# Three entries moved in a hand-written instruction order: a product of decays, a cumulative sum and a store in the fifth unit's stage

## The chip, the cores and the metric

The kernel runs on one core of a Trainium2 chip. The metric is the device time of one execution in microseconds (us). Before the change the median of three runs is 170.76 us, from 170.74 to 170.88 us.

## The reference, cut to what matters

For 4 batches and 8 heads a 48 by 48 state is carried over 768 tokens; every row of the state decays by its own factor alpha. The result, 3072 tokens of 384 numbers, goes through two matrix products with a squared ReLU between them.

```
state = alpha[:, :, t, :, None] * state + einsum('bhd,bhe->bhde', k[:, :, t], v[:, :, t])
y[:, :, t] = einsum('bhd,bhde->bhe', q[:, :, t], state)
...
h = x @ w_in            # 3072 x 384 by 384 x 2048
g = relu(h) * relu(h)
out = g @ w_out         # 2048 x 384
```

## The kernel before, in words

The work is cut into 12 units of 256 tokens each: `units` runs over three stretches of the sequence, and within a stretch over the four batches. Units are numbered from 0, so the fifth unit is unit 4 and the sixth is unit 5. A partition holds two neighbouring tokens. Names of operations end in the unit's number.

A unit's **front** (from unit 2 on, `decays_by_pair`) works as follows. Four loads bring alpha, k, q and v (`lda`, `ldk`, `ldq`, `ldv`, line 463). VectorE, or GpSimd for some units, multiplies the alphas of a token pair (`pr`, L570). ScalarE takes the logarithm of the product (`ln`, L573) and of the odd token's alpha (`lm`, L612). TensorE sums the logarithms over the tokens (`m1i`, a triangular matrix, L579, and four small matmuls, L582) into the bank `psW`, the first of the three banks of `psWH`. ScalarE takes three exponentials of that bank (`ei` L590, `ea` L592, `ec` L595); VectorE makes the other token's factors from them (`bk` L599, `lb` L614), ScalarE one more exponential (`es`, L616). VectorE multiplies k and q by the factors (`ekm` L646, `eqm0` and `eqm1` L641), into the tile `qks`. Two DMA transposes on SyncE's queue (`tr0`, `tr1`, L657) write the transposed tile `kqt`.

The **attention** part is one group on TensorE that makes the scores and the state's increment (`p0`, L877 and L730), two masked copies on VectorE (`mk`, L894) and a group for the output (`y`, L757 and L765). ScalarE and VectorE copy the output to the tile `xbf` (`xe` L911, `xf` L913). It is transposed (`xt`: for units 0 to 3 by TensorE, L929, with a copy to the tile `xt` on VectorE, `xv` L941, the "mix copy" here, or on ScalarE, L943; from unit 4 on by a DMA, L935).

The **dense** part makes eight groups of 12 matmuls for a unit's first layer (`s1_unit_0` to `_7`, L992). Their results go in turn to two banks, so that each group needs the copy of the group two before it to be done. That copy is the ReLU (`re`, L1000 on ScalarE or L1002 on VectorE), and the squares follow (`sq`, L1010, L1013, L1014). The second layer has two rows of tokens of four groups of four matmuls (`s2_unit_row_0` to `_3`, L1038), gathered in the bank `psO`, copied out by `oe` (L1045, L1047) to the tile `osb` and stored by `out` (L1054).

The order on each engine is written out by hand in `TABLES`, one list of names for each engine. `arrange` takes the operations in exactly this order, and `place` sets semaphore waits where an operation needs a result of another engine or of a DMA. An engine works through its list in order; it does not pass an instruction that waits. Which bank or buffer a group uses is set where the operation is made and not by its place in the list.

The place of the change is the stretch in which unit 2's dense part begins, unit 1's second layer ends and unit 4's front is made. There ScalarE's list reads `... xf2 xe2 lm4 ln4 vc3 ei4 ea4 ec4 re2_0 re2_1 es4 oe1_0 ...` (`vc3` copies unit 3's v to bf16, L637). The kernel ends with the last unit's second layer (`last_tile`, L953) and its stores.

Of the kernel before, what the change touches and what calls it, by code (L numbers as in the profile page):

```python
# [26 lines left out]
class Program:  # L27
# [145 lines left out]
    def emit(self):  # L173
# [48 lines left out]
        zero zlinc zlstr zident zcaus zcaus1 zla0 zla1 zones zown zown0 zown1 zqk0 zqk1 zqk2 zlb0 zlb1 ekm0_0  # L222
        eqm0_0 ekm1_0 eqm1_0 et10_0 mk0_0 sa0 mk1_0 ekm1 eqm0_1 eqm1_1 xv0 et1_1 sc0 mk1_1 mk0_1 sc1 re0_2 xf1
        sq0_3 xv1 pr2 sq0_5 re0_7 re1_0 lb2 re1_1 ekm2 eqm0_2 eqm1_2 sq0_7 re1_5 et1_2 sq1_1 sq1_5 re1_7 mk1_2
        pr3 sc2 mk0_2 lb3 eqm1_3 eqm0_3 ekm3 xv2 pr4 sq1_7 bk4 lb4 ekm4 eqm1_4 eqm0_4 sq2_1 mk1_3 mk0_3 sc3
        oe1_1 sd3 sq2_7 sq2_6 xf3 lb5 ekm5 eqm1_5 eqm0_5 sa4 mk1_4 mk0_4 re3_2 pr6 sc4 sq3_1 xf4 sq3_3 re3_5
        sq3_6 lb6 ekm6 sa5 mk0_5 sc5 mk1_5 eqm0_6 eqm1_6 oe3_0 xf5 sq4_1 re4_5 pr7 sq4_3 sq4_7 sq4_5 bk7 lb7
        eqm0_7 sa6 eqm1_7 ekm7 sc6 sd6 mk0_6 mk1_6 pr8 oe4_1 xf6 sq5_3 bk8 lb8 ekm8 sq5_5 sq5_6 sa7 mk0_7 sc7
# [8 lines left out]
        +256 +256 tr01_0 p0_0 tr11_0 kv0 +512 +512 +512 +256 +256 p1_0 m11 +512 +256 y0 +512 +512 +256 tr0_1 xt0  # L237
        tr1_1 s1_0_0 p0_1 s1_0_1 s1_0_3 s1_0_2 s1_0_4 y1 s1_0_5 xt1 s1_0_6 s1_0_7 s1_1_0 m1i2 s1_1_1 s1_1_2
        s1_1_3 s1_1_4 s1_1_5 tr0_2 s1_1_6 tr1_2 s2_0_0_0 s1_1_7 p0_2 s2_0_0_1 s2_0_0_2 s2_0_1_0 s2_0_1_1 m1i3
        s2_0_1_2 s2_0_0_3 s2_0_1_3 y2 s2_1_0_0 s2_1_0_1 xt2 s2_1_0_2 s1_2_0 s1_2_1 m1i4 s2_1_0_3 s1_2_2 s1_2_3  # L240
        s2_1_1_0 s1_2_4 s2_1_1_1 s1_2_5 p0_3 s2_1_1_2 s1_2_6 s1_2_7 s2_1_1_3 y3 m1i5 s2_2_0_0 s2_2_0_1 xt3
        s2_2_0_2 s2_2_0_3 s1_3_0 p0_4 s2_2_1_0 s2_2_1_1 s2_2_1_2 s2_2_1_3 s1_3_2 s1_3_1 y4 s1_3_4 s1_3_3 m1i6
        s1_3_6 s1_3_5 s2_3_0_0 s2_3_0_1 s1_3_7 p0_5 s2_3_0_2 s1_4_0 s1_4_1 s2_3_0_3 s1_4_2 s1_4_3 y5 s2_3_1_0
# [15 lines left out]
        vc10  # L259
    """,  # L260
    "sp": """
        lda0 ldk0 ldq0 ldv0 lda1 ldk4 ldq4 tr0_3 tr1_3 lda5 ldv4 tr0_4 tr1_4 out0_1 ldv5 lda6 ldk6 tr1_5 out1_1
        tr0_5 xt4 ldq6 ldv6 lda7 ldq7 ldk7 tr0_6 tr1_6 out2_1 xt5 ldv7 lda8 ldk8 out3_1 tr0_7 tr1_7 out4_1 xt6
        ldq8 ldv8 lda9 ldq9 ldk9 tr0_8 tr1_8 xt7 ldv9 lda10 out5_1 ldk10 tr0_9 tr1_9 out6_1 xt8 ldq10 ldv10
        lda11 ldk11 tr0_10 tr1_10 out7_1 xt9 ldq11 ldv11 tr0_11 tr1_11 xt10 out8_1 xt11 out9_1 out10_1 out11_0
# [852 lines left out]
```

## Time and profile before

| What | Before |
|---|---|
| Median of three runs | 170.76 us (170.74 to 170.88) |
| The profiled execution's own time | 171.26 us |
| Its span, first to last instruction | 169.5 us |
| Time outside the span | 1.76 us |
| TensorE matmuls, share of the span | 163.8 us, 97% |
| VectorE | 118.0 us, 70% |
| ScalarE | 109.6 us, 65% |
| GpSimd | 35.3 us, 21% |
| Granted TensorE clock | 1.0 of full speed |

A profile shows one execution. "PE" is TensorE, "PEld" its weight loads, "DVE" VectorE, "ACT" ScalarE, "POOL" GpSimd, "SP" SyncE; "SPq" and "POOLq" are rows in which the engine's queue issues a DMA. In a row of the timeline stand the start in us from the span's start, the duration, the engine, the line of the code, the operation with what it writes and reads, and in square brackets the idle time of the engine just before it with what ended it. Matmuls overlap in the pipeline: a row's duration reaches past the start of the next one, so lost time on TensorE is read from start to start. A DMA's landing is its start and the time to landing that the list of DMA issues gives.

### The profile page before, as it was taken

What the parts mean: (1) busy time and instruction counts of PE and PEld (TensorE: products, weight loads), DVE (VectorE), ACT (ScalarE), POOL (GpSimd) and SP (SyncE); (2) the same over time, 40 slices, a digit from 0 to 9 for tenths busy, and PEclk for the clock granted to TensorE, in tenths of its full rate; (3) what the DMA queues carried; (4) which work ended last, traced back from release to release, by engine and by line L of the source; (5) the groups of instructions that cost most, each with busy time, mean ns of one, the idle gap of its engine ahead of it and who ended that gap; (6) DMA issues with size and microseconds to landing.
All of it is one profiled execution on the core that took longest, in us unless ns stands there. A gap on an engine that the chain in (4) does not pass through costs nothing.

```text
span 169.5 us, 5392 instructions
## 1 busy us (share of the span) xinstructions
PE 163.8 (97%) x2369; PEld 125.9 (74%) x2369; DVE 118.0 (70%) x206; ACT 109.6 (65%) x212; POOL 35.3 (21%) x46
## 2 busy tenths in 40 slices
PE   7988999999799999999999999999999999999994
PEld 2556889767686697877778876788797788787773
DVE  6577899985849868975978977887969637342130
ACT  3968778786868388667477757375677374466440
POOL 4671879130172032100240000000600000000000
DMA  5999999989999998999989999979797761040012
GB/s 137 324 318 188 260 312 215 293 288 252 185 220 329 241 181 197 307 137 243 301 195 247 263 152 258 207 194 288 145 190 205 97 119 58 0 141 4 33 60 93
DMA packets 68407, 33.37 MB, mean 197 GB/s; under 512 B 63520, under 2 KB 65312, under 8 KB 68384
## 3 DMA queue, kind: packets, MB, share of 16 engines
q1 hardware_dynamic: 62784, 24.39, 65.6%
q0 software_dynamic: 3520, 7.87, 18.6%
q10 hardware_dynamic: 2080, 0.79, 1.8%
q8 instruction: 18, 0.29, 0.7%
q14 instruction: 5, 0.04, 0.1%
HBM read 25.17 MB, written 4.72 MB: 176 GB/s over the span
## 4 chain that ended last, share of the span: by engine, by line
PE 83%; DMA 12%; ACT 1%; POOL 1%; issue 1%; DVE 0%; SPq 0%
PE psO L1038 34%; PE psWH L992 33%; DMA raw<-in_alpha_dram 6%; DMA raw<-in_v_dram 3%; DMA raw<-in_k_dram 2%; PE psX L877 2%; PE psZ L765 2%; PE psX L953 2%; PE psWH L1038 2%; PE psWH L730 1%; PE psZ L877 1%; PE psX L765 1%; PE psO L992 1%; PE psWH L579 1%; POOL raw L463 1%; ACT rr L1000 1%
## 5 line engine op out<-in xcount | busy, mean ns | idle before, releaser
L992 PE MATMUL psWH<-xt,win 128*128 128x256 bf16 x552 | 70.5, 273 | 0.9 <-ACT rr L1000 0.9
L1038 PE MATMUL psO<-wout,gt 128*128 128x384 bf16 x352 | 67.0, 326 | 0.0
L992 PEld LDWEIGHTS psWH<-xt,win 128*128 128x128 bf16 x552 | 59.8, 114 | 7.4 <-ACT rr L1000 1.4
L1000 ACT ACTIVATE rr<-psWH 128x512 bf16<-128x512 f32 x79 | 46.5, 599 | 25.3 <-PE psWH L992 24.0
L1038 PEld LDWEIGHTS psO<-wout,gt 128*128 128x128 bf16 x352 | 32.7, 98 | 16.7 <-DVE gt L1010 0.2
L1010 DVE TENSOR_TENSOR gt<-rr 128x1024 bf16<-128x1024 bf16 (+1 forms) x46 | 26.6, 584 | 22.4 <-ACT rr L1000 22.4
L1013 POOL TENSOR_TENSOR gt<-rr 128x1024 bf16<-128x1024 bf16 x3 | 5.7, 1911 | 56.6 <-ACT rr L1000 56.6
L894 DVE TENSOR_TENSOR pm<-psZ,caus 128x1024 bf16<-128x1024 f32 x12 | 14.6, 1216 | 3.7 <-PE psWH L730 3.0
L1045 ACT ACTIVATE osb<-psO 128x384 f32<-128x384 f32 x17 | 8.4, 492 | 11.6 <-PE psO L1038 11.2
L894 DVE TENSOR_TENSOR pm<-psX,caus 128x1024 bf16<-128x1024 f32 x12 | 14.6, 1215 | 0.9 <-PE psX L877 0.5
L641 DVE TENSOR_TENSOR qks<-raw,eq 128x384 bf16<-128x384 f32 x22 | 11.4, 550 | 1.1 <-ACT eq L616 1.0
L646 DVE TENSOR_TENSOR qks<-raw,ek 128x768 bf16<-128x768 f32 x11 | 10.5, 950 | 1.1 <-ACT ek L558 1.0
L1002 DVE TENSOR_SCALAR rr<-psWH 128x512 bf16<-128x512 f32 x13 | 8.8, 683 | 1.2 <-PE psWH L992 1.2
L1014 ACT ACTIVATE gt<-rr 128x512 bf16<-128x512 bf16 (+1 forms) x11 | 8.9, 821 | 0.6 <-DVE rr L1002 0.4
L573 ACT ACTIVATE lab<-prd 128x384 bf16<-128x384 f32 x10 | 5.2, 522 | 6.0 <-DVE prd L570 5.8
L1086 PE MATMUL psO<-zero 128*128 128x512 bf16 (+1 forms) x27 | 7.7, 418 | 1.3 <-DVE zero L382 1.3
L913 DVE CAST xbf<-psZ 128x384 bf16<-128x384 f32 x10 | 5.5, 554 | 3.4 <-PE psZ L757 3.2
L850 POOL TENSOR_TENSOR sbd<-tmp,acm 128x192 bf16<-128x192 f32 x5 | 2.9, 588 | 20.6 <-DVE tmp L840 16.2
L911 ACT ACTIVATE xbf<-psX 128x384 bf16<-128x384 f32 x11 | 5.4, 490 | 2.4 <-PE psZ L757 2.3
L637 ACT ACTIVATE vbf<-raw 128x768 bf16<-128x768 f32 x7 | 5.9, 837 | 1.2 <-DMA raw<-in_v_dram 1.2
L570 DVE TENSOR_TENSOR prd<-raw 128x384 f32<-128x384 f32 x9 | 6.4, 707 | 0.2 <-DMA raw<-in_alpha_dram 0.2
L616 ACT ACTIVATE eq<-la 128x384 f32<-128x384 f32 x10 | 5.2, 522 | 2.0 <-DVE la L614 2.0
(130 smaller groups left out, 190.8 us busy)
## 6 DMA issues: line engine op xcount, KB each, us to landing
out_dram<-osb SPq DMA_DIRECT2D x11, 384.0 KB, 3.3
raw<-in_alpha_dram SPq DMA_DIRECT2D x9, 384.0 KB, 5.5
raw<-in_v_dram SPq DMA_DIRECT2D x9, 384.0 KB, 4.4
raw<-in_k_dram SPq DMA_DIRECT2D x8, 384.0 KB, 5.7
raw<-in_q_dram SPq DMA_DIRECT2D x8, 384.0 KB, 4.0
win<-in_moe_w_in_dram POOLq DMA_DIRECT2D x4, 384.0 KB, 8.8
wout<-in_moe_w_out_dram POOLq DMA_DIRECT2D x4, 384.0 KB, 8.9
raw<-in_k_dram POOLq DMA_DIRECT2D x3, 384.0 KB, 6.4
```

Of the source, the lines that this page charges most:

```text
L570: add("dve", lambda e: e.tensor_tensor(hd(PRD[la][:]), al(0), al(1), ALU.mult), dve_ns(HD), p0, reads=[("raw", r, 0)], writes=[("prd", la) ...
L641: add("dve", lambda e, j=j, dst=dst: e.tensor_tensor(dst, RAW[r][:, 2, :, j, :].rearrange("p (n x) d -> p n x d", x=2), EQ[la][:, j].rearr ...
L646: add("dve", lambda e, a=a, E=E: e.tensor_tensor(QKS[qs][:, a, :, :, 0:D], RAW[r][:, 1 + a].rearrange("p h j d -> p j h d"), E[la][:].rear ...
L894: add("dve", lambda e, hf=hf, psT=psT: e.tensor_tensor(PM[pm][:, hf].rearrange("p r n j t -> p (r n) (j t)"), psT[:, :, :].rearrange("p r ...
L992: ins = pe.matmul(psN[:, i * T:(i + 1) * T], WIN[:, kk, hidden(fj)], mov, start=(kk == 0), stop=(kk == KT - 1))
L1000: add("act", lambda e, psN=psN, rr=rr: e.activation(rr, psN, AF.Relu), act_ns(512), pu + 600, reads=[keyN], writes=[("rr", rb, half)], nam ...
L1002: alts={"dve": (lambda e, psN=psN, rr=rr: e.tensor_scalar(rr, psN, 0.0, None, ALU.max), dve_ns(512))})
L1010: add("dve", lambda e, dst=dst, sq=sq: e.tensor_tensor(dst, sq, sq, ALU.mult), 148 + k * 267, pu + 1200, reads=[("rr", rb, h) for h in ran ...
L1014: "act": (lambda e, dst=dst, sq=sq: e.activation(dst, sq, AF.Square), act_ns(k * 512))})
L1038: ins = pe.matmul(psS, GT[gt][:, fj, j, :], WOUT[:, fj, :], start=(fj == 0), stop=(fj == FT - 1))
L1045: add("act", lambda e, j=j, psS=psS: e.activation(OSB[ob][:, j], psS, AF.Copy), act_ns(DM), ps_ + 700, reads=[keyS], writes=[("osb", ob, j ...
L1086: pr.arrange(TABLES, lambda n: lambda pe: pe.matmul(psO[:, 0:n], ZERO[:, 0:128], ZERO[:, 0:n], skip_group_check=True), zero)
```

## The change

Three names change their places in `TABLES`. Nothing else is different: the same operations run on the same engines with the same buffers.

```
 dve:
-  ... eqm0_3 ekm3 xv2 pr4 sq1_7 bk4 lb4 ...
+  ... eqm0_3 ekm3 pr4 xv2 sq1_7 bk4 lb4 ...
 pe:
-  ... xt2 s2_1_0_2 s1_2_0 s1_2_1 m1i4 s2_1_0_3 s1_2_2 s1_2_3 ...
+  ... xt2 s2_1_0_2 m1i4 s1_2_0 s1_2_1 s2_1_0_3 s1_2_2 s1_2_3 ...
 sp:
-  ... tr0_3 tr1_3 lda5 ldv4 tr0_4 tr1_4 out0_1 ldv5 lda6 ...
+  ... tr0_3 tr1_3 lda5 out0_1 ldv4 tr0_4 tr1_4 ldv5 lda6 ...
```

On TensorE, behind the transposes of unit 2's output (L929) and a second-layer group, the difference of the two orders reads as follows; the rows with `lab0` are `m1i4`, the twelve matmuls from `xt2` are `s1_2_0` and `s1_2_1`, and those behind them `s1_2_2` and `s1_2_3`.

```order
 L929 MATMUL psX<-ident,xbf0 128x2x64 x6
 L1038 MATMUL psO<-wout,gt1 128x384 x4
-L992 MATMUL psWH<-xt2,win 128x256 x12
 L579 MATMUL psWH<-lab0,linc 128x384
 L582 MATMUL psWH<-ones2,lab0 128x2 x4
+L992 MATMUL psWH<-xt2,win 128x256 x12
 L1038 MATMUL psO<-wout,gt1 128x384 x4
 L992 MATMUL psWH<-xt2,win 128x256 x12
```

The cumulative sum now stands ahead of two groups of unit 2's first layer, which stood ahead of it.

On VectorE, behind unit 3's products with q and k, `prd0` from `raw0` is `pr4`, and the copy to `xt2` is `xv2`.

```order
 L641 TENSOR_TENSOR qks0<-raw3,eq1 128x4x2x48 x2
 L646 TENSOR_TENSOR qks0<-raw3,ek1 128x16x48
+L570 TENSOR_TENSOR prd0<-raw0 128x384
 L941 COPY xt2<-psX 128x768
-L570 TENSOR_TENSOR prd0<-raw0 128x384
 L1010 TENSOR_TENSOR gt1<-rr3 128x512
 L599 TENSOR_TENSOR ek0<-ek0,raw0 128x384
```

The two have changed places.

On SyncE's queue the rows run from unit 3's two transposes to the load of unit 6's alpha. `raw1` from alpha is `lda5`, `raw0` from v is `ldv4`, the transposes to `kqt1` are unit 4's, and the row with `osb0` is the first store, `out0_1`.

```order
 L657 DMA_TRANSPOSE kqt0<-qks0 128x16x64 x2
 L463 DMA raw1<-in_alpha_dram 128x8x96
+L1054 DMA out_0_dram<-osb0 128x768
 L463 DMA raw0<-in_v_dram 128x8x96
 L657 DMA_TRANSPOSE kqt1<-qks1 128x16x64 x2
-L1054 DMA out_0_dram<-osb0 128x768
 L463 DMA raw1<-in_v_dram 128x8x96
 L463 DMA raw2<-in_alpha_dram 128x8x96
```

The store has moved ahead of one load and the fifth unit's two transposes. The lists of ScalarE and GpSimd are the same as before.

More of the change, by code (lines that the diff above doesn't have):

```diff
@@ L224 @@
         sq0_3 xv1 pr2 sq0_5 re0_7 re1_0 lb2 re1_1 ekm2 eqm0_2 eqm1_2 sq0_7 re1_5 et1_2 sq1_1 sq1_5 re1_7 mk1_2
-        pr3 sc2 mk0_2 lb3 eqm1_3 eqm0_3 ekm3 xv2 pr4 sq1_7 bk4 lb4 ekm4 eqm1_4 eqm0_4 sq2_1 mk1_3 mk0_3 sc3
+        pr3 sc2 mk0_2 lb3 eqm1_3 eqm0_3 ekm3 pr4 xv2 sq1_7 bk4 lb4 ekm4 eqm1_4 eqm0_4 sq2_1 mk1_3 mk0_3 sc3
         oe1_1 sd3 sq2_7 sq2_6 xf3 lb5 ekm5 eqm1_5 eqm0_5 sa4 mk1_4 mk0_4 re3_2 pr6 sc4 sq3_1 xf4 sq3_3 re3_5
@@ L239 @@
         s1_1_3 s1_1_4 s1_1_5 tr0_2 s1_1_6 tr1_2 s2_0_0_0 s1_1_7 p0_2 s2_0_0_1 s2_0_0_2 s2_0_1_0 s2_0_1_1 m1i3
-        s2_0_1_2 s2_0_0_3 s2_0_1_3 y2 s2_1_0_0 s2_1_0_1 xt2 s2_1_0_2 s1_2_0 s1_2_1 m1i4 s2_1_0_3 s1_2_2 s1_2_3
+        s2_0_1_2 s2_0_0_3 s2_0_1_3 y2 s2_1_0_0 s2_1_0_1 xt2 s2_1_0_2 m1i4 s1_2_0 s1_2_1 s2_1_0_3 s1_2_2 s1_2_3
         s2_1_1_0 s1_2_4 s2_1_1_1 s1_2_5 p0_3 s2_1_1_2 s1_2_6 s1_2_7 s2_1_1_3 y3 m1i5 s2_2_0_0 s2_2_0_1 xt3
@@ L261 @@
     "sp": """
-        lda0 ldk0 ldq0 ldv0 lda1 ldk4 ldq4 tr0_3 tr1_3 lda5 ldv4 tr0_4 tr1_4 out0_1 ldv5 lda6 ldk6 tr1_5 out1_1
+        lda0 ldk0 ldq0 ldv0 lda1 ldk4 ldq4 tr0_3 tr1_3 lda5 out0_1 ldv4 tr0_4 tr1_4 ldv5 lda6 ldk6 tr1_5 out1_1
         tr0_5 xt4 ldq6 ldv6 lda7 ldq7 ldk7 tr0_6 tr1_6 out2_1 xt5 ldv7 lda8 ldk8 out3_1 tr0_7 tr1_7 out4_1 xt6
```

## The prediction

> **What bounds the kernel now.** I read the page's shares first, then the waits of TensorE alone, then the timeline at the change. The page's busy times:
>
> ```profile
> PE 163.8 (97%) x2369; PEld 125.9 (74%) x2369; DVE 118.0 (70%) x206; ACT 109.6 (65%) x212; POOL 35.3 (21%) x46
> ```
>
> TensorE is busy for 97% of the span, so only time that TensorE itself loses can be won. The view of the waits, TensorE alone (total, times, longest; its first three rows):
>
> ```profile
> PE psO L1086 <- DVE zero L382: 1.3, 1, 1.3
> PE psWH L992 <- ACT rr L1000: 0.9, 1, 0.9
> PE psZ L669 <- DVE qks L646: 0.5, 1, 0.5
> ```
>
> The 1.3 us are the start of the program and the 0.5 us unit 2's transposes; the 0.9 us, one wait of the first layer for a ReLU on ScalarE, are the only long wait after them. The timeline of TensorE shows where they lie:
>
> ```profile
> 39.32 0.50 PE L929 MATMUL psX<-ident,xbf 128*128 128x128 bf16 x6
> 39.66 0.81 PE L1038 MATMUL psO<-wout,gt 128*128 128x384 bf16 x4
> 40.47 1.50 PE L992 MATMUL psWH<-xt,win 128*128 128x256 bf16 x12
> 41.81 0.33 PE L579 MATMUL psWH<-lab,linc 128*128 128x384 bf16 x1
> 41.98 0.24 PE L582 MATMUL psWH<-ones,lab 128*128 128x2 bf16 x4
> 42.08 0.81 PE L1038 MATMUL psO<-wout,gt 128*128 128x384 bf16 x4
> 43.74 1.50 PE L992 MATMUL psWH<-xt,win 128*128 128x256 bf16 x12 [0.85 <-ACT rr L1000]
> ```
>
> They are: xt2, s2_1_0_2, then s1_2_0 with s1_2_1, m1i4, s2_1_0_3, and s1_2_2 with s1_2_3. What holds s1_2_2 is re2_0, the ReLU that frees its bank. ScalarE at that time:
>
> ```profile
> 38.97 0.54 ACT L612 ACTIVATE la<-raw 128x384 f32<-128x384 f32 x1
> 40.91 0.53 ACT L573 ACTIVATE lab<-prd 128x384 bf16<-128x384 f32 x1 [1.40 <-DVE prd L570]
> 41.35 0.83 ACT L637 ACTIVATE vbf<-raw 128x768 bf16<-128x768 f32 x1
> 42.25 0.49 ACT L590 ACTIVATE ek<-psWH 128x384 f32<-128x384 f32 x1
> 42.64 0.48 ACT L592 ACTIVATE eq<-psWH 128x384 f32<-128x384 f32 x1
> 43.01 0.18 ACT L595 ACTIVATE acm<-psWH 128x8 f32<-128x8 f32 x1
> 43.07 0.62 ACT L1000 ACTIVATE rr<-psWH 128x512 bf16<-128x512 f32 x1
> ```
>
> These are lm4, ln4, vc3, ei4, ea4, ec4, re2_0. ScalarE sits idle 1.40 us for pr4, and then works without a pause to re2_0, which ends at 43.69; s1_2_2 starts at 43.74. ei4 starts just after m1i4 ends (41.98 + 0.24 = 42.22) and just after vc3 ends (42.18), so both have to come sooner. VectorE explains the 1.40 us:
>
> ```profile
> 38.09 0.95 DVE L646 TENSOR_TENSOR qks<-raw,ek 128x768 bf16<-128x768 f32 x1
> 39.86 0.56 DVE L941 COPY xt<-psX 128x768 bf16<-128x768 bf16 x1 [0.82 <-PE psX L929]
> 40.33 0.55 DVE L570 TENSOR_TENSOR prd<-raw 128x384 f32<-128x384 f32 x1
> ```
>
> pr4 (40.33) stands behind xv2, which waits 0.82 us for xt2 on TensorE (39.32 + 0.50 = 39.82). pr4 needs only the alphas, and lm4 reads those same alphas at 38.97.
>
> **The change, part by part.**
>
> *pr4 ahead of xv2.* ekm3 ends at 39.04. pr4 fits into the idle 0.82 us: about 39.0 to 39.55, ahead of the 39.82 at which xv2 could start at the earliest. So xv2 costs nothing more; if pr4 had to wait for its data, xv2 could be at most pr4's 0.55 us late. Then ln4 follows lm4 (end 39.51) at about 39.55 to 40.08, 1.36 us sooner, and vc3 about 39.99 to 40.82.
>
> *m1i4 ahead of s1_2_0.* How long four second-layer matmuls hold TensorE, I read from eight in a row:
>
> ```profile
> 53.86 1.46 PE L1038 MATMUL psO<-wout,gt 128*128 128x384 bf16 x8
> 55.16 0.82 PE L992 MATMUL psWH<-xt,win 128*128 128x256 bf16 x6
> 55.91 0.42 PE L877 MATMUL psX<-kqt 64*64 64x128 bf16 x16
> ```
>
> Eight take 55.16 - 53.86 = 1.30 us from start to start, so four take 0.65. From 39.66 TensorE is therefore free at 40.31, but s1_2_0 started at 40.47 because xv2 ended at 40.42: 0.16 us lost. In the same way s2_1_0_3, at 42.08, leaves TensorE free at 42.73, and s1_2_2 started at 43.74: 1.01 us lost. Now m1i4 takes the place at 40.32, with lab4 ready at 40.08, and holds TensorE for 0.27 us (42.08 - 41.81), the same as before. s1_2_0 then starts at 40.59, behind xv2's 40.42: the wait of 0.16 us is covered by work that has to be done anyway. s1_2_0 and s1_2_1 take 1.34 us (41.81 - 40.47), so s2_1_0_3 starts at 41.93 and s1_2_2 can start at 42.58.
>
> *Is re2_0 in time?* m1i4's last matmul ends 0.41 us after its start, at 40.73; vc3 ends at 40.82. Then ei4 starts at about 40.8, 1.45 us sooner. From ei4's start to re2_0's end were 43.69 - 42.25 = 1.44 us, so re2_0 ends near 42.25. s1_2_0, which it reads, ends at about 41.4, ahead of re2_0's start near 41.6. re2_0 is 0.33 us ahead of s1_2_2's 42.58. The hole closes: 43.74 - 42.58 = 1.16 us, or 1.01 + 0.16 = 1.17 from the two losses.
>
> *What is late next?* The rest of ScalarE's and VectorE's chain there (es4, oe1_0, bk4, lb4) comes about 1.4 us sooner, more than TensorE does. Behind it TensorE's groups follow each other and wait for engines that wait for TensorE, so they move along. What does not move is what a DMA brings. The first such point is unit 3's p0_3:
>
> ```profile
> 47.78 0.42 PE L877 MATMUL psX<-kqt 64*64 64x128 bf16 x16
> ```
>
> Its second transpose landed at 40.78 + 4.1 = 44.9 (rows below); p0_3 would now begin at 46.61, late enough. The next is unit 4's p0_4, at 55.91 before (above) and 54.74 now.
>
> *The store ahead of ldv4, tr0_4 and tr1_4.* SyncE's queue, and the time to landing of tr1_3, lda5, tr1_4 and out0_1, one view each:
>
> ```profile
> 40.78 1.65 SPq L657 DMA_TRANSPOSE kqt<-qks  x1
> 42.48 1.23 SPq L463 DMA_DIRECT2D raw<-in_alpha_dram  x1
> 43.75 0.64 SPq L463 DMA_DIRECT2D raw<-in_v_dram  x1
> 45.63 3.85 SPq L657 DMA_TRANSPOSE kqt<-qks  x2
> 49.52 0.69 SPq L1054 DMA_DIRECT2D out_dram<-osb  x1
> ```
>
> ```profile
> 48.15 1.32 SPq L657 DMA_TRANSPOSE kqt<-qks  x1
> ```
>
> ```profile
> kqt<-qks SPq DMA_TRANSPOSE x1, 4.1
> ```
>
> ```profile
> raw<-in_alpha_dram SPq DMA_DIRECT2D x1, 384.0 KB, 5.7
> ```
>
> ```profile
> kqt<-qks SPq DMA_TRANSPOSE x1, 5.6
> ```
>
> ```profile
> out_dram<-osb SPq DMA_DIRECT2D x1, 384.0 KB, 5.4
> ```
>
> Before, tr1_4 landed at 48.15 + 5.6 = 53.7, 2.2 us ahead of p0_4, and the store at 54.9, 1.2 us after it. Now the store is issued at 43.75 for 0.69 us, and ldv4 behind it ends at about 45.1. The fifth unit's `qks`, ready at 45.6 before, is ready at about 44.2 since lb4 comes sooner, so the transposes are issued at about 45.15, 0.5 us sooner than before, but with a store's 1.2 us of transfer ahead of them. The landing of tr1_4 lies between 53.7 - 0.5 = 53.2, if the store goes into gaps, and 53.7 + 1.2 = 54.9, if it is paid in full. A gap is there, in this row of busy times by stretch (the last three columns are TensorE's granted clock, the busy share of the DMA engines, and GB/s):
>
> ```profile
> 48.00:49.00 1.00, 1.00 (x67) 0.84 (x56) 0.26 (x1) 0.74 (x3) 0.71 (x1) 1.00 0.51 27
> ```
>
> The DMA engines are free for half of that 1 us, ahead of tr1_4's landing. Against 54.74 this costs 0 to 0.2 us; I take 0, since the middle of the two landings, 54.05, is early enough.
>
> [...] Priced in full, the sum would be 1.0 us instead of 1.17.
>
> The store's move also takes away a wait that the gain could make: oe2_0, on ScalarE shortly before p0_4, rewrites the buffer that the store reads, and would come 1.17 us nearer to the store's old landing at 54.9. With the store landed some five microseconds sooner that cannot hold. ldv4 lands up to 1.2 us later; its copy is needed only by p0_4. Later loads have the same transfers ahead of them as before.
>
> *Sum.* 1.17 us off the profiled execution: 171.26 - 1.17 = 170.09 us. That execution was 0.50 us above the median of the runs; taken off the median 170.76, the forecast is **169.6 us**.
>
> **The rivals.**
>
> *Part of the gain is given back to a load that does not move.* lda5 is issued at 42.48 in both orders and landed at 48.2. On it hang pr5 (POOL), and behind that ln5 and m1i5:
>
> ```profile
> 48.29 1.00 POOL L572 TENSOR_TENSOR prd<-raw 128x384 f32<-128x384 f32 x1 [0.33 <-DMA raw<-in_alpha_dram]
> 51.27 0.52 ACT L573 ACTIVATE lab<-prd 128x384 bf16<-128x384 f32 x1
> ```
>
> With everything 1.17 us sooner ln5 comes at 50.10, 0.8 us behind pr5's end (49.29). If the store right behind lda5 delayed it by its 1.2 us, pr5 would end at 50.5, ln5 would be 0.4 us late, and m1i5, which waits for it on TensorE, about as much: 170.0 us. With the 0.2 us of p0_4 as well: 170.2 us. Against it: lda5 stands ahead of the store.
>
> *The wait only changes its place.* If lab4 or vc3 is late, ei4 is, and re2_0 with it. All 1.17 us would be lost only if ScalarE gained nothing, with pr4 held to its old time by its data; then 170.8 us. lm4's start at 38.97 without a pause speaks against it.
>
> *Slower: the transposes behind the store.* The point is p0_4's old start. Once tr1_4 lands after 54.74 the gain shrinks, after 55.9 the kernel is slower than before. A store ahead of the transposes costs them at most its whole time from issue to landing, for which the page has a median over eleven stores:
>
> ```profile
> out_dram<-osb SPq DMA_DIRECT2D x11, 384.0 KB, 3.3
> ```
>
> 53.7 + 3.3 = 57.0 would be 1.1 us behind p0_4's old start: 171.9 us, and 171.4 us with the 0.5 us of earlier issue taken off. For it: the queue is one, and the store stands ahead of the transposes. Against it: before, the store landed only 1.2 us after the transpose ahead of it, so most of the 3.3 us runs beside other transfers.
>
> **How the numbers follow.** 0.65 for the forecast, 169.4 to 169.9 (0.1 us is the reading of the rows, and 0.2 the landing of tr1_4). 0.15 for a part given back, 169.9 to 170.4. 0.09 for a wait that changes its place, to 171.1. 0.11 for the transposes, 171.1 to 171.9. The range 169.3 to 170.5 takes in the first two cases and the edge of the third. A measurement of this kernel can tell about 0.2%, 0.34 us, from no change: faster is below 170.42. Faster 0.79, same 0.09, slower 0.12.
>
> **What would show it.** Right: pr4 near 39.0, ln4 near 39.55, no idle time of ScalarE for pr4; m1i4 near 40.3; s1_2_2 near 42.6 with no wait for a ReLU; ln5 near 50.1 and p0_4 near 54.7; a span of 169.5 - 1.2 = 168.3 us. Wrong: a wait of p0_4 for `kqt`, of m1i5 for `lab`, or of s1_2_0 for a late xv2. A gain that is seen at 43 us and gone at 56 us would speak for the DMA, and one that never appears for ScalarE.

## The result, and the profile after

| | Before | After |
|---|---|---|
| Median of 17 executions | 170.95 us (170.65 to 172.11) | 173.74 us (170.99 to 175.59) |
| The profiled execution's own time | 171.26 us | 170.99 us |
| Its span | 169.5 us | 169.3 us |
| p0_2 to p0_4, from start to start | 24.29 us | 24.41 us |
| p0_4 to TensorE's end | 111.28 us | 111.28 us |

The kernel became slower: after to before is 1.0075, with a 95% interval of 1.0049 to 1.0102, and the forecast of 169.6 us, from 169.3 to 170.5, was wrong. That ratio leaves out the executions that lie over 1.5% above their kernel's fastest, nine of the changed kernel's 17, though here it is the change that makes them long; the two medians alone are 1.6% apart.

The profiled execution of the changed kernel is its shortest of the 17. It ends 0.27 us sooner than the profile of before only because it began better: p0_2 starts at 31.24 and not at 31.62. From p0_2 on it has lost 0.12 us. So this profile shows that the gain is gone, and not yet why the median is 2.8 us higher; an experiment's profile of the same kernel (e10, below) shows that.

The hole that was to be closed is closed. TensorE of the changed kernel, with m1i4 (L579), s1_2_0 and s1_2_1, s2_1_0_3, and s1_2_2:

```profile
39.93 0.33 PE L579 MATMUL psWH<-lab,linc 128*128 128x384 bf16 x1
40.20 1.48 PE L992 MATMUL psWH<-xt,win 128*128 128x256 bf16 x12
41.52 0.81 PE L1038 MATMUL psO<-wout,gt 128*128 128x384 bf16 x4
42.17 1.04 PE L992 MATMUL psWH<-xt,win 128*128 128x256 bf16 x8
```

s1_2_2 starts 0.65 us after s2_1_0_3, with nothing between them. ScalarE at that place: lm4, ln4, and behind ec4 the two ReLUs re2_0 and re2_1.

```profile
38.59 0.54 ACT L612 ACTIVATE la<-raw 128x384 f32<-128x384 f32 x1
39.17 0.52 ACT L573 ACTIVATE lab<-prd 128x384 bf16<-128x384 f32 x1
...
41.19 1.12 ACT L1000 ACTIVATE rr<-psWH 128x512 bf16<-128x512 f32 x2
```

ln4 follows lm4 with no idle time, where it waited 1.40 us before. The waits of TensorE in the changed kernel (total, times, longest):

```profile
PE psO L1086 <- DVE zero L382: 1.2, 1, 1.2
PE psX L877 <- DVE qks L641: 1.1, 1, 1.1
```

The wait for the ReLU is gone from the second row, and p0_4's wait stands in its place. The timeline has it after six matmuls of the first layer:

```profile
53.71 0.82 PE L992 MATMUL psWH<-xt,win 128*128 128x256 bf16 x6
55.65 0.42 PE L877 MATMUL psX<-kqt 64*64 64x128 bf16 x16 [1.12 <-DVE qks L641]
```

Such six matmuls hold TensorE for 0.75 us from start to start (55.16 to 55.91 before). p0_4 was due at 54.46 and started at 55.65: 1.19 us lost, a little more than the 1.07 us won by then (24.29 us less the 23.22 from 31.24 to 54.46). The releaser that the row names, VectorE's product `qks`, had been done for some ten microseconds (tr0_4, which reads it, was issued at 45.74); what came last is the transpose of it. SyncE's queue, the store L1054 ahead of ldv4 and of both transposes, and then tr1_4 alone with its time to landing:

```profile
43.94 1.27 SPq L1054 DMA_DIRECT2D out_dram<-osb  x1
45.26 0.44 SPq L463 DMA_DIRECT2D raw<-in_v_dram  x1
45.74 5.19 SPq L657 DMA_TRANSPOSE kqt<-qks  x2
```

```profile
49.60 1.33 SPq L657 DMA_TRANSPOSE kqt<-qks  x1
```

```profile
kqt<-qks SPq DMA_TRANSPOSE x1, 6.0
```

tr1_4 lands at 49.60 + 6.0 = 55.6, at p0_4's start. Before it was issued at 48.15 and landed at 53.7. tr0_4 was issued 0.1 us later than before, but issuing it held SyncE for 49.60 - 45.74 = 3.86 us instead of about 2.5.

What the DMA engines did meanwhile is in the busy times by stretch (after the five engines: the granted clock, the DMA engines' busy share, and GB/s):

```profile
51.00:52.00 1.00, 1.00 (x8) 0.54 (x7) 0.93 (x3) 1.00 (x4) 0.97 (x1) 1.00 1.22 311
52.00:53.00 1.00, 1.00 (x12) 0.80 (x11) 0.56 (x1) 0.42 (x2) 1.00 (x2) 1.00 2.98 300
53.00:54.00 1.00, 1.00 (x9) 0.69 (x7) 0.85 (x1) 0.92 (x3) 0.11 (x1) 1.00 0.30 6
54.00:55.00 1.00, 0.53 (x5) 0.26 (x3) 0.49 (x2) 0.84 (x2) 0.00 (x0) 1.00 0.76 171
```

Some 310 GB/s flow until nearly 53, then 6 GB/s for a whole microsecond, with the transposes in flight. The DMA engines are not out of work. The share of 2.98 in the stretch ahead says so: the time of a packet is counted where it begins, and 22 of the transposes' packets of 256 bytes, begun from 52.94 to 53.07, lasted from 1.36 to 1.50 us. I call this a **standstill**. In the trace these 22 all end together, from 54.42 to 54.46.

### The profile page after: what moved, and what is told of

It reads as the page before. It is cut to its first block, busy times and chain, and to the rows that moved or that the text cites. A ratio compares the mean times of both kernels' runs of the same rounds, so it can differ in the third digit from the quotient of the medians.

```text
span 169.3 us, 5390 instructions
## 1 busy us (share of the span) xinstructions
PE 163.3 (96%) x2367; PEld 126.4 (75%) x2369; DVE 118.0 (70%) x206; ACT 109.7 (65%) x212; POOL 35.5 (21%) x46
## 4 chain that ended last, share of the span: by engine, by line
PE 84%; DMA 10%; DVE 2%; ACT 1%; POOL 1%; issue 0%; SPq 0%
PE psWH L992 35%; PE psO L1038 32%; DMA raw<-in_q_dram 5%; DMA raw<-in_v_dram 3%; DMA raw<-in_k_dram 2%; PE psX L877 2%; PE psZ L765 2%; PE psO L992 2%; PE psX L953 2%; PE psWH L1038 2%; PE psWH L730 1%; PE psZ L877 1%; PE psX L765 1%; PE psWH L579 1%; PE psZ L669 1%; POOL raw L463 1%
## 5 line engine op out<-in xcount | busy, mean ns | idle before, releaser
L1013 POOL TENSOR_TENSOR gt<-rr 128x1024 bf16<-128x1024 bf16 x3 | 5.7, 1896 | 55.3 <-ACT rr L1000 55.3
L877 PE MATMUL psX<-kqt 64*64 64x128 bf16 x192 | 5.0, 222 | 1.4 <-DVE qks L641 1.1
```

The source lines that it names most:

```text
L877: ins = pe.matmul(psT[64 * c:64 * c + 64, rr_, o:o + 128], keys, mov)
```

## The experiments

Each was run beside the kernel before on the same chip, with 6 to 12 executions to a median; a ratio is to that kernel before, with its 95% interval.

### Which of the three moves costs: e1 to e4

e1 makes the store's move alone.

```
 sp:
-  lda5 ldv4 tr0_4 tr1_4 out0_1
+  lda5 out0_1 ldv4 tr0_4 tr1_4
```

> Only the store moves, ahead of ldv4 and the fifth unit's transposes; pr4 and m1i4 stay where they were. Store theory (the store ahead of the transposes makes them land late): tr1_4 lands 1 to 2 us later than the 53.7 us of before, at 54.7 us or later, which is near or past p0_4's old start at 55.9 us; the time is 0 to 2 us longer than before, and the 1 us hole ahead of s1_2_2 is still there. Rival, demand theory (p0_4 is due sooner and unit 5's two loads on ScalarE's queue are issued sooner, since everything ahead of them moved, and these push the transposes back): nothing moved that would make this happen, so tr1_4 lands within 0.5 us of 53.7 and the time is that of before within 0.2%.

Measured: 173.27 us (170.99 to 175.21), ratio 1.0102 (1.0070 to 1.0134). The store's move alone makes the whole loss. Its profiled execution is once more its shortest: without the other two moves p0_4 is due later, and tr1_4, which landed at 55.56, 1.85 us later than before, was just in time. TensorE goes from the six matmuls to p0_4 without a wait:

```profile
54.88 0.82 PE L992 MATMUL psWH<-xt,win 128*128 128x256 bf16 x6
55.65 0.42 PE L877 MATMUL psX<-kqt 64*64 64x128 bf16 x16
```

That p0_4 waits in e1's longer executions is not shown, since none of them was profiled.

e2 makes the other two moves and leaves the store where it was.

```
 dve:  ... eqm0_3 ekm3 pr4 xv2 ...
 pe:   ... xt2 s2_1_0_2 m1i4 s1_2_0 s1_2_1 s2_1_0_3 ...
 sp:   as before
```

> pr4 and m1i4 move as in the change, the store stays behind the fifth unit's transposes. Store theory: the hole ahead of s1_2_2 closes, tr1_4 lands at 53.7 us or sooner, p0_4 starts near 54.7 us without a wait, and the time is 1.0 to 1.2 us shorter than before (about 0.65%). Demand theory: p0_4 waits for the transposes as in the changed kernel, 1 us or more, and the time is that of before or longer.

Measured: 170.38 us (169.44 to 172.36), ratio 0.9964 (0.9934 to 0.9994). Its p0_4 does not wait:

```profile
53.98 0.82 PE L992 MATMUL psWH<-xt,win 128*128 128x256 bf16 x6
54.73 0.42 PE L877 MATMUL psX<-kqt 64*64 64x128 bf16 x16
```

From p0_2 to p0_4 are 23.07 us against 24.29 before: 1.22 us won, where the forecast had 1.17. tr1_4 landed at 53.2. The profiled execution took 170.09 us, 1.17 less than that of before; the medians, beside the kernel before on the same chip, are only about 0.7 us apart. Where the longer executions of e2 lose the rest no profile shows.

e3 makes only VectorE's move (`pr4` ahead of `xv2`), e4 that and the store's.

```
 dve:  ... eqm0_3 ekm3 pr4 xv2 ...
 pe:   as before
 sp:   e3 as before;  e4  lda5 out0_1 ldv4 tr0_4 tr1_4
```

> Only pr4 moves ahead of xv2. Both theories: ln4 starts near 39.6 instead of 40.91 us, but ei4 still waits for m1i4, which ends at 42.22 us, so the hole ahead of s1_2_2 stays about 1 us and the time is that of before within 0.2%. A gain of over 0.3 us here would say that vc3 and not m1i4 held ei4.

> pr4 and the store move, m1i4 does not. Store theory: as with the store alone, 0 to 2 us longer than before, with tr1_4 landing 1 us or more later than before. Demand theory: that of before within 0.2%, since TensorE and the loads on ScalarE's queue come when they came.

Measured: e3 170.89 us, ratio 0.9992 (0.9976 to 1.0008); e4 172.99 us (172.49 to 174.82), ratio 1.0131 (1.0090 to 1.0171). The product's move by itself does nothing that can be measured; the gain needs the cumulative sum's, which was not tried without the product's. The profile of e4 is a long execution, 174.82 us, and shows what the profile of after could not. p0_4 waits, and the clock falls (busy times by stretch, TensorE's first; the granted clock is the third column from the end):

```profile
PE psX L877 <- DMA kqt<-qks: 2.3, 1, 2.3
```

```profile
54.49:57.89 3.40, 1.19 (x10) 0.76 (x7) 1.61 (x3) 1.58 (x4) 0.00 (x0) 1.00 1.29 154
57.89:61.30 3.41, 3.36 (x71) 2.33 (x72) 1.83 (x3) 0.00 (x0) 0.00 (x0) 0.50 1.19 320
61.30:64.71 3.41, 3.41 (x55) 2.58 (x55) 1.74 (x3) 1.20 (x3) 0.00 (x0) 1.00 0.79 203
```

After a stretch in which TensorE worked for 1.19 of 3.40 us, the next 3.41 us run at half the clock. From p0_4 to TensorE's end e4 took 112.81 us and before 111.28: 1.53 us more.

### The change again, in a long execution: e10

e10 is the changed kernel itself.

```
 the change, as it is
```

> The changed kernel itself, beside the other two on the same chip. Store theory: p0_4 waits for the fifth unit's transposes for 1 us or more, by a different amount from execution to execution; where it waits longest, the granted clock of TensorE falls to half for about 3.4 us after the wait; the time is 0.5 to 1.5% longer than before. If the wait is there but the clock stays at 1.0 in the profile, the profile shows the wait alone, and the time of that execution is within 0.3% of before.

Measured: 173.51 us (171.77 to 175.96), ratio 1.0090 (1.0052 to 1.0128). Its profiled execution took 175.96 us. Its wait, and p0_4:

```profile
PE psX L877 <- DMA kqt<-qks: 3.5, 1, 3.5
```

```profile
53.49 0.82 PE L992 MATMUL psWH<-xt,win 128*128 128x256 bf16 x6
57.85 0.64 PE L877 MATMUL psX<-kqt 64*64 64x128 bf16 x16 [3.54 <-DMA kqt<-qks]
```

The DMA engines stood still twice, from 51 to 53 and for about a microsecond up to 56.7, and the clock fell behind it:

```profile
51.00:52.00 1.00, 1.00 (x10) 0.62 (x8) 0.87 (x3) 0.81 (x3) 0.00 (x0) 1.00 0.15 41
52.00:53.00 1.00, 1.00 (x12) 0.68 (x10) 0.40 (x1) 0.61 (x1) 0.00 (x0) 1.00 0.24 44
...
55.00:56.00 1.00, 0.00 (x0) 0.00 (x0) 0.91 (x1) 0.00 (x0) 0.06 (x1) 1.00 1.85 92
56.00:57.00 1.00, 0.00 (x0) 0.00 (x0) 0.22 (x2) 0.00 (x0) 0.00 (x0) 0.92 0.51 107
```

```profile
53.43:56.84 3.41, 0.88 (x8) 0.56 (x6) 0.96 (x2) 1.27 (x3) 1.63 (x2) 1.00 1.30 179
56.84:60.25 3.41, 2.40 (x68) 1.87 (x69) 1.89 (x4) 0.00 (x0) 0.00 (x0) 0.50 1.18 322
60.25:63.67 3.42, 3.42 (x12) 1.61 (x11) 1.75 (x2) 0.00 (x0) 0.00 (x0) 0.50 1.13 275
```

The second standstill ended 0.8 us behind a packet of the queue that the list of DMA queues calls "instruction" (54.88 to 55.84); what that means is taken up under e13 to e18.

Wait and clock account for the whole: against the profile of before, p0_2 comes 0.45 us sooner (31.17), p0_2 to p0_4 takes 26.68 instead of 24.29 us (2.39 more), and p0_4 to TensorE's end 114.03 instead of 111.28 (2.75 more, behind 6.83 us at half the clock). 2.39 + 2.75 - 0.45 = 4.69 us, which is the difference of the spans, 174.21 - 169.52.

### Is it the store's bytes, or its queue: e5, e9, e6

In e5 and e9, the same kernel twice, the moved store writes only the first 48 of 768 numbers of each partition; the rest of that block of the output is left out.

```
+ w = 48 if g == 0 else 2 * DM
- e.dma_start(dst, OSB[ob][:]...)
+ e.dma_start(dst[:, 0:w], OSB[ob][:]...[:, 0:w])
```

> The changed kernel, with the first store cut to 48 of its 768 numbers per partition, in its new place; the rest of those 256 rows of the output is left out. Bytes theory (the store's 393 KB of transfer, ahead of the transposes on the same DMA engines, is what makes them late): tr1_4 lands near 53.5 us as without the store, p0_4 does not wait, and the time is that of the kernel with only pr4 and m1i4 moved, 0.2 to 0.7% shorter than before. Rival, place theory (a store of any size between loads and transposes on the queue holds the transposes up): tr1_4 lands at 55 us or later, and the time is 0.5% or more longer than before.

> The changed kernel with the first store cut to 48 of its 768 numbers per partition (the rest of those 256 rows of the output is left out), once more, for a profile at the common speed of the chip. Bytes theory: tr1_4 lands near 53.5 us, within 0.7 us of where it lands with only pr4 and m1i4 moved. Place theory: at 55 us or later, with a wait of p0_4 of 0.5 us or more.

Measured: e5 171.55 us, ratio 0.9986 (0.9956 to 1.0015), its profile taken in an execution of 417 us and not read here; e9 171.9 us (170.03 to 175.19), ratio 1.0009 (0.9978 to 1.0041). Against e10, run with e9 on one chip, a sixteenth of the bytes gives back 0.8%; taking the store away gives 1.1% (1.0075 to 0.9964), and the longest executions are as long as those of the change. The profile of e9 shows one of 173.22 us, with the same wait of 3.5 us, though the small store had landed at 47.6:

```profile
50.00:51.00 1.00, 1.00 (x36) 0.77 (x30) 1.00 (x4) 1.00 (x4) 0.00 (x0) 1.00 2.12 55
51.00:52.00 1.00, 1.00 (x10) 0.60 (x8) 0.87 (x3) 0.84 (x4) 0.00 (x0) 1.00 0.07 20
52.00:53.00 1.00, 1.00 (x12) 0.71 (x10) 0.43 (x1) 0.58 (x1) 0.29 (x1) 1.00 0.92 101
```

So the bytes are a part of the price at most, and a standstill and a wait as long as those of the whole store come without them too. Neither theory came out: tr1_4 landed at 57.8 in this execution, as the place theory had it, but neither ratio is 0.5% above 1.

e6 issues the moved store on ScalarE's queue instead, behind `oe1_0`.

```
 sp:
-  lda5 out0_1 ldv4 tr0_4 tr1_4
+  lda5 ldv4 tr0_4 tr1_4
 act:
-  oe1_0 re2_2
+  oe1_0 out0_1 re2_2
```

> The changed kernel, with the first store issued from ScalarE's queue behind oe1_0, near 43 us, and not from SyncE's: it is no longer in the ring of the transposes, but is as many bytes at the same time. Bytes theory: the transposes are nearly as late as in the change (tr1_4 lands at 54.5 us or later) and the time is that of before or longer. Ring theory (only what stands ahead in the same queue holds the transposes up): tr1_4 lands near 53.5 us, and the time is 0.2 to 0.7% shorter than before.

Measured: 171.71 us (171.03 to 171.9), ratio 1.0025 (1.0008 to 1.0042). tr1_4, with no store ahead of it in its own queue, landed at 56.2, and p0_4 waited 0.7 us. That is the bytes theory's forecast, and the ring theory missed: another queue did not take the store out of the transposes' way here (53.2 without the store's move, in e2). The time has a second loss in it. p0_3 waited 1.0 us, with a ReLU named that had ended 0.4 us before; unit 3's second transpose, issued at 40.9 and still under way when the store was issued at 42.4, landed at 47.25, and at 45.05 in e2.

### The transposes first: e7 and e8

e7 keeps the other two moves and puts the store and ldv4 behind the transposes.

```
 sp:
-  lda5 out0_1 ldv4 tr0_4 tr1_4
+  lda5 tr0_4 tr1_4 ldv4 out0_1
```

> pr4 and m1i4 moved as in the change; on SyncE's queue the fifth unit's transposes come first, straight behind lda5, and ldv4 and then the store behind them. Both theories of the store (bytes or ring): one transfer less ahead of the transposes than before, so tr1_4 lands 0.5 to 1.5 us sooner than the 53.2 us with only pr4 and m1i4 moved, p0_4 has about 2 us to spare, and the time is 1.0 to 1.2 us shorter than before in all runs (about 0.65%). If the transposes are late here too, what holds them is not what stands ahead of them.

Measured: 170.54 us (170.14 to 170.88), ratio 0.9973 (0.9955 to 0.9990): faster than both kernels, and with the smallest scatter of all. tr1_4 landed at 52.3 and p0_4 had 2.2 us to spare, as expected; the gain is 0.4 us and not 1.0 to 1.2, and where the rest goes is not shown.

```profile
53.81 0.82 PE L992 MATMUL psWH<-xt,win 128*128 128x256 bf16 x6
54.56 0.42 PE L877 MATMUL psX<-kqt 64*64 64x128 bf16 x16
```

e8 is e7 with one more exchange: on GpSimd `bk5` ahead of `vc4`, since in e7 `bk5` stood behind `vc4`'s wait for ldv4.

```
 pool:
-  pr5 vc4 bk5 sd4
+  pr5 bk5 vc4 sd4
```

> As with the transposes first, and on GpSimd bk5 stands ahead of vc4, since there vc4 waited until 53.2 us for the late ldv4 and held bk5, and with it unit 5's products and transposes, by about 2 us. Store theory with this chain: bk5 runs near 52 us again, unit 5's first transpose is issued near 55.3 instead of 57.0 us, p0_4 and p0_5 both have 2 us to spare, and the time is 1.0 to 1.2 us shorter than before (about 0.65%), against 0.4 us with the transposes first alone. Rival (the 0.4 us are lost in another place than bk5): the time is that of the transposes first alone, within 0.2%.

Measured: 170.79 us (170.05 to 173.08), ratio 1.0000 (0.9974 to 1.0025): a miss. bk5 did run sooner (52.63 instead of 54.02), and vc4 then waited for ldv4 alone. The profiled execution took 172.04 us, one of the longer ones, and was late already at p0_2 (32.37, and 31.50 in e7). In it ldv4 landed at 54.6 and the store at 56.9 (53.2 and 54.1 in e7); p0_4 waits for the copy of v, and a second-layer group for `oe2_0`, which waits for the store's landing:

```profile
PE psO L1038 <- ACT osb L1045: 0.8, 1, 0.8
...
PE psX L877 <- POOL vbf L636: 0.3, 1, 0.3
```

### All transfers on one queue: e11 and e12

Unit 5's loads of k and q are issued on ScalarE's queue, beside the transposes. e11 is the changed kernel with both on SyncE's queue.

```
-ACT_LOADS = {5: "kq"}
+ACT_LOADS = {}
 sp:
-  lda5 out0_1 ldv4 tr0_4 tr1_4
+  lda5 out0_1 ldk5 ldv4 ldq5 tr0_4 tr1_4
```

> The changed kernel, with unit 5's two loads of k and q taken from ScalarE's queue to SyncE's, in the order lda5 out0_1 ldk5 ldv4 ldq5 tr0_4 tr1_4: the same transfers ahead of the fifth unit's transposes as landed ahead of them in the change's late execution, but all in one queue. The bytes theory has fallen with the small store, which delayed them as much. Two-queue theory (the DMA engines stand still for 1 to 3 us where the transposes of SyncE's queue and loads of ScalarE's queue are on them at the same time, and the store pushes the transposes into those loads): without a second queue no packet of the stretch takes over 1 us, tr1_4 lands at 53 to 54.3 us, and p0_4 starts near 54.5 us with a wait of 0.3 us at most; the time is 0.3 to 0.7% shorter than before. Place theory (anything more ahead of the transposes delays them): tr1_4 lands at 55.5 us or later, p0_4 waits 1 us or more, and the time is that of before or longer.

Measured: 171.04 us (170.52 to 171.99), ratio 1.0000 (0.9984 to 1.0015). The long executions are gone: the longest is 172.0 us. The rest is what the place theory forecast, and the two-queue theory missed each of its numbers: tr1_4 landed at 55.7, p0_4 waited 1.5 us, there is a standstill with one queue too, and the gain is used up:

```profile
PE psX L877 <- DMA kqt<-qks: 1.5, 1, 1.5
```

```profile
53.00:54.00 1.00, 1.00 (x10) 0.76 (x8) 1.00 (x2) 0.92 (x3) 0.00 (x0) 1.00 1.32 18
```

e12 has one queue too, with the store behind the transposes and between unit 5's loads.

```
 sp:
-  lda5 out0_1 ldv4 tr0_4 tr1_4 ldv5
+  lda5 ldv4 tr0_4 tr1_4 ldk5 out0_1 ldq5 ldv5
```

> A try for a better version: pr4 and m1i4 moved as in the change, unit 5's loads of k and q on SyncE's queue, in the order lda5 ldv4 tr0_4 tr1_4 ldk5 out0_1 ldq5 ldv5. Two-queue theory: tr1_4 lands at 51 to 52 us without a standstill, p0_4 has 2 us or more to spare, ldq5 lands near 55 us and makes unit 5's products up to 1 us late, which p0_5 has to spare; the time is 1.0 to 1.2 us shorter than before, with less scatter than with only pr4 and m1i4 moved. Place theory: the same landing to within 1 us of the 53.2 us that only pr4 and m1i4 gave, and the time 0.2 to 0.5% shorter than before.

Measured: 172.46 us (170.6 to 174.42), ratio 1.0035 (1.0004 to 1.0066). Both theories forecast a gain and missed. p0_4 did not wait (tr1_4 landed at 51.4), but the store landed at 56.6, and the wait has moved to the group behind `oe2_0`, which rewrites the buffer that the store reads:

```profile
PE psO L1038 <- ACT osb L1045: 1.8, 1, 1.8
```

### What stands behind a standstill: e13 to e18

The queue that the list of DMA queues calls "instruction" carried 18 packets, 0.29 MB, in the profiled executions of before and after, 16 KB each. In the changed kernel one falls amid the transposes, as the list of DMA queues for 52.4 to 52.9 us shows (packets, MB, share):

```profile
q1 hardware_dynamic: 450, 0.11, 97.7%
q8 instruction: 1, 0.02, 14.1%
```

It began at 52.54 and ended at 53.66, the standstill 0.80 us later. Between tr1_4's issue and its landing such a packet begins in the profiles of after (52.5), e11 (52.5), e12 (51.0), e6 (54.0), e9 (54.8), e1 (54.9), e10 (54.9) and e4 (55.1); there is none in before (54.6), e3 (54.7), e2 (53.5, just behind the landing), e7 (53.8) and e8 (53.9). In e1, e4, e9 and e10 the packet lies about where it lies in before, and meets the transposes because they are late already. In e4, e9 and e10 they then stand until 0.8 us behind it, which makes them later still; in e1 tr1_4 landed before that. To move the packet, six kernels cut the filler matmuls that TensorE runs early in the program into more pieces, with the same columns in all, so that TensorE has taken more instructions by unit 4. e13 and e15 do so to e2, with 33 and 79 matmuls more; e14, e16, e17 and e18 to the changed kernel, with 79, 103, 111 and 119 more. Each brings a weight load (2369 matmuls and 2369 loads in the profile of before), so the instructions are twice as many.

```
 pe:
-  +512 ... +512
+  +128 +128 +128 +128 ...        (e13: eleven of them)
+  +104 +102 +102 +102 +102 ...   (e14, e15: all; e16 to e18 finer still)
```

> pr4 and m1i4 moved, store at its old place (the version that gained 0.4%), and 11 of the filler matmuls of 512 columns at the start cut into four of 128: 66 more instructions on TensorE (with their weight loads), the same filler columns. Fetch theory (a 16 KB packet of the instruction queue, which comes at set places of TensorE's program, holds the transposes that are under way until about 0.8 us after it): the packet that came at 53.5 us, just behind tr1_4's landing, comes near 50 to 51 us, a standstill of over 1 us ends 0.8 us behind it, tr1_4 lands at 54.2 us or later instead of 53.2, p0_4 waits in many executions, and the time is 0.3 to 1.0% longer than without the added instructions, about that of before or up to 0.6% above it. Rival (the packets and the standstills only happen together): tr1_4 lands near 53.2 us and the time stays 0.3 to 0.6% shorter than before.

> The changed kernel with all the fillers of 512 columns at the start cut into five and seven of those of 256 into two: 158 more instructions on TensorE. Fetch theory: the packet that came at 52.5 us (amid the transposes) comes at 46 to 48.5 us, ahead of them, and the next not before p0_4's start; the standstill that ended at 54.5 us is gone, tr1_4 lands 1 to 1.5 us sooner than 55.55 us, at 54.0 to 54.6 us, and the time is 0.5% or more shorter than that of the change, so between 0.6% shorter and 0.4% longer than before. Rival: it is as late as in the change, and the time is 0.6% or more longer than before.

> The version with only pr4 and m1i4 moved, with the same 158 instructions more at the start. Fetch theory: no packet of the instruction queue can meet the fifth unit's transposes, tr1_4 lands at 53.2 us or sooner in nearly all executions, the scatter (169.4 to 172.4 us without them) shrinks to about 1 us, and the time is 0.5 to 0.8% shorter than before. Rival: time and scatter as without the added instructions, 0.1 to 0.6% shorter.

| | Packet begins | tr1_4 lands | p0_4 waits | Time, ratio |
|---|---|---|---|---|
| e2 | 53.5 | 53.2 | 0 | 170.38 us, 0.9964 (0.9934 to 0.9994) |
| e13 | 51.8 | 55.6 | 0.4 | 171.75 us, 1.0046 (1.0017 to 1.0074) |
| e15 | 50.1 | 55.6 | 1.0 | 172.14 us, 1.0030 (0.9996 to 1.0063) |
| after | 52.5 | 55.6 | 1.1 | 173.74 us, 1.0075 (1.0049 to 1.0102) |
| e14 | 50.0 | 55.3 | 0.4 | 172.1 us, 1.0047 (1.0021 to 1.0073) |

e14 and e15 missed their aim: the packet went from behind the transposes, or from their end, to their middle. Neither came out faster than before; e14's time lies between the fetch theory's and its rival's. As it fell out, e13 and e15 are the test without the store's move. Two kernels whose transfers stand in e2's order, with the packet moved in among the transposes, land tr1_4 2.4 us later than e2 and lose what e2 gains; of the 2.4 us, 0.6 in e13 and 0.4 in e15 are a later issue of tr1_4. e13's profile, an execution near its median, is 1.8 us longer than e2's, and p0_4's wait of 0.4 us is the smaller part of that: 0.5 us is lost ahead of p0_2, which the finer fillers may cost, and 0.8 us behind p0_4, where a second-layer group waits for `oe2_0`, and that for the store, which landed at 56.7 and at 54.3 in e2.

```profile
57.37 1.31 PE L1038 MATMUL psO<-wout,gt 128*128 128x384 bf16 x7 [0.78 <-ACT osb L1045]
```

e15's profile is one of its longer executions. It has the same 0.8 us, and its clock falls to half behind them. Its standstill is where the packet is (it ended 0.88 us after it):

```profile
50.00:51.00 1.00, 1.00 (x47) 0.89 (x47) 0.94 (x4) 1.00 (x4) 0.00 (x0) 1.00 2.81 153
51.00:52.00 1.00, 1.00 (x10) 0.60 (x7) 1.00 (x3) 1.00 (x4) 0.20 (x1) 1.00 0.08 9
```

The other half of the test, the store ahead and the packet out of the way, was tried three times more.

> The whole change, with its early filler matmuls cut into more pieces, same columns, so that 206 more TensorE instructions run ahead of 40 us; nothing else is changed. With 158 more the instruction packet that fell at 52.5 us in the change came at 50.0, still amid the fifth unit's transposes. Theory that an instruction packet amid the transposes is half of the loss: if the packets now fall near 45 and after 54.5, the second transpose lands by 54.5, p0_4 waits 0 to 0.3 us and the time is 0.995 to 1.000 of before. If a packet still falls between 47 and 53: as the change, 1.004 to 1.010. Theory of the store alone: 1.007 wherever the packet falls.

> The same with 222 more instructions, about 0.7 us further. Fetch theory: a packet near 45 and the next near 55, 0.995 to 1.000, p0_4 waits under 0.3 us. Store theory: 1.007.

> The same with 238 more instructions. Fetch theory: a packet near 44 and the next near 53.5, at the end of the transposes, 0.998 to 1.004. Store theory: 1.007. All three theories' times include what the finer fillers may cost by themselves, at most the 0.3 us by which the kernels with 158 more differed from their parents at p0_2.

Measured: e16 173.18 us, ratio 1.0113 (1.0068 to 1.0157); e17 171.96 us, 1.0079 (1.0050 to 1.0108); e18 172.59 us, 1.0079 (1.0051 to 1.0108). None of them got the packet out: it began at 49.7, 50.5 and 53.4, each time ahead of tr1_4's landing (56.9, 56.2 and 56.6). e18's packet came where it was aimed, and the fetch theory's time for that, 0.998 to 1.004, was missed; the store theory's 1.007 lies within all three intervals. But the finest fillers also cost something themselves, more than the 0.3 us allowed: p0_2 started at 32.0 to 32.45 us, and at 31.24 in after. And the loss is not in one place: in e17 p0_4 did not wait at all, and TensorE stood for 1.2 us in m1i5 for a reason that its profile does not name.

Two things speak against taking the packet for the whole cause. In e14 and e16, where it began near 50 among the transposes, the DMA engines slowed behind it and did not stop: 176 and 155 GB/s flowed from 51 to 52. And in e1, where none met the transposes before tr0_4 had landed at 54.8, tr1_4 still landed 1.85 us later than before, with 130 to 186 GB/s from 50 to 53. So in that profile the store's move makes the transposes late without a packet among them; how much of the loss would remain in the whole change, and in its longer executions, stays open.

## Why the prediction was wrong, point by point

- **pr4 ahead of xv2, m1i4 ahead of s1_2_0: right.** ln4 lost its idle time, the wait for the ReLU went, and the two moves alone (e2) won 1.22 us up to p0_4, where the sum had 1.17. The rivals of a wait that changes its place on ScalarE, and of a late lda5, did not come: lda5 landed at 47.6 in the changed kernel, sooner than before.
- **The store ahead of the transposes, costed at 0 to 0.2 us: this is the step that failed.** The prediction put tr1_4's landing between 53.2 and 54.9. It was 55.6 in the best execution and 57.8 in a bad one, and the store's move alone made the kernel 1.0% slower (e1). Three terms were wrong in it.
  - *The gap was no gap.* The row of 48 to 49 us before, with half of the DMA engines' time free at 27 GB/s, was read as room for the store. In that microsecond ldv4 and tr0_4 were issued and had not landed (they did at 49.3 and 51.9): work was there, and almost nothing moved. It was a standstill: 19 of the transposes' packets in flight, which lasted from 0.97 to 1.49 us, ended together from 49.17 to 49.21. In the stretches around it 241 to 321 GB/s flow, so there was no room, and the store's 1.2 us were paid in full and more: tr1_4 landed 1.85 us later in e1 than before.
  - *The transposes were not issued sooner.* They were to come 0.5 us sooner, at 45.15. The products were ready, at 43.7, but the store's issue held SyncE's queue for 1.27 us, where the sum had 0.69, and tr0_4 was issued at 45.74, 0.1 us later than before. tr1_4 came 1.45 us later than before, since the issue of tr0_4 took so much longer. Why it does is not shown; it took 3.8 to 5.1 us in the profiles with the whole store close ahead of it in its queue (after, e1, e4, e10), and 2.5 to 2.8 us in before, e2 and e3.
  - *A standstill was not thought of.* The changed kernel's transposes met an instruction packet and stood until 54.46. e13 and e15, without the store's move, have a landing some 2 us later with such a packet among the transposes.
- **The rival "slower: the transposes behind the store" had the right wait, p0_4's for the transposes, at 0.11 and 171.1 to 171.9 us; both its chance and its price were too low.** Its price ended at a landing of 57.0 us, with the store's 3.3 us from issue to landing as the most that it could cost. Not in it were a landing of 57.8 (e10) and the clock that was halved behind the wait, which cost another 1.5 us (e4) and 2.75 us (e10).
- **The other price, the store paid in full, pointed the right way and should have weighed more than the gap.** It put tr1_4's landing at 54.9, and it was 55.6. The landings before follow the order of issue (lda5 48.2, ldv4 49.3, tr0_4 51.9, tr1_4 53.7, out0_1 54.9), and with the store ahead of the transposes e11's do so too: lda5 47.3, out0_1 48.4, ldk5 49.6, ldv4 51.1, ldq5 52.3, tr0_4 54.9, tr1_4 55.7. e6 and e9 show that this order isn't the whole price: there the store was in another queue or small, and tr1_4 landed at 56.2 and 57.8.

The loss is thus shown to be the store's move (e1 alone loses it, e2 without it gains), paid in the profiles of the changed kernel as a late tr1_4 at p0_4 and, in the long one, as half a clock behind it. That an instruction packet amid the transposes can put them back further is supported without the store's move by e13 and e15; e14 and e16 show that it need not stop them. Open is what makes the longer standstill of 50 to 53 us in e10 and e9: no instruction packet is near it, and packets of SyncE's and ScalarE's queues stand still in it alike. It is absent where unit 5's loads share SyncE's queue (e11), but also in the short execution of the changed kernel, where they don't; that these loads cause it is argued from one profile and from e11's smaller scatter, not shown, and e12, with one queue too, ran at 122 to 148 GB/s from 48 to 52 us.

## What to carry to other kernels

A low rate in a stretch of the profile was no free room here: 27 GB/s flowed from 48 to 49 us before, with ldv4 and tr0_4 issued and not yet landed, and with the store moved ahead tr1_4 landed 1.85 us later (e1). Look at what is in flight before a transfer is put there. A transfer that a matmul waits for goes ahead of one that nobody waits for, and a margin of two microseconds at its landing is not too much when the DMA engines are busy: e7 had 2.2 us and executions from 170.1 to 170.9, e2 had 1.5 us and executions from 169.4 to 172.4. Take the price of a late transfer from a bad execution and not from the profiled one alone: here waits of 2.3 and 3.5 us on TensorE were followed by another 1.5 and 2.75 us in clock.

## What the runs showed of the hardware that was not expected

- The DMA engines stood still with work in flight: 6 GB/s for a microsecond in after, 9 in e15, about 42 for two in e10. Of the eight standstills in the trace of after six ended 0.79 to 0.90 us behind an instruction packet of 16 KB (54.46 is one) and two about 1.7 us behind one. The one at 49.21 in before, which the prediction took for a gap, has none near it: the last had ended at 46.78.
- The granted clock fell to 0.50 for 3.41 us (e4), 6.83 us (e10) and 3.41 us (e15), behind stretches of 3.4 us in which TensorE worked for 1.19, 0.88 and 1.59 us, 35%, 26% and 47% of them; in e15 the wait for the transposes was 1.0 us and that for `oe2_0` 0.8. A wait of 3.5 us need not do it: in e9's profile p0_4 waited as long as in e10, and the granted clock stayed at 1.0. The clock's changes in e4, at 57.89, 61.30 and 173.94, lie a multiple of 3.41 us apart. Counted in such steps from the change behind e9's last instruction (172.15), an estimate, e9's wait falls in two stretches, with 1.65 us of work in each. First e15, then e9:

```profile
54.08:57.49 3.41, 1.59 (x71) 1.25 (x69) 1.85 (x4) 0.66 (x2) 0.00 (x0) 1.00 1.13 322
57.49:60.91 3.42, 3.42 (x12) 1.57 (x11) 1.80 (x2) 0.32 (x1) 0.00 (x0) 0.50 1.31 240
```

```profile
52.69:56.10 3.41, 1.65 (x13) 1.05 (x10) 0.96 (x1) 2.05 (x4) 1.79 (x2) 1.00 1.47 181
56.10:59.51 3.41, 1.65 (x70) 1.32 (x71) 1.72 (x4) 0.00 (x0) 0.00 (x0) 1.00 1.01 268
```

So two waits of 3.5 us had different prices in clock, nothing in e9 and 6.83 us at half the clock in e10: the length alone does not settle it. That it depends on where the wait falls among such stretches is an estimate from these five; where the line lies they do not show.
- A store of a sixteenth of the bytes, in front of the transposes, can be followed by the same wait of 3.5 us as the whole one (e9 and e10).
